# A forward loop in two-step order, halved products, writes moved to SyncE, and leftover work spread over the steps

## The chip, the cores and the metric

The kernel runs on one core of a Trainium2 chip, in one launch. The metric is the device time of that launch in microseconds, the median of several runs. One execution was also taken with the hardware profiler; its times are those of the tables and lines below. The engines are named as in the profile: PE (TensorE, matmuls), PEld (its weight loads), DVE (VectorE), ACT (ScalarE), POOL (GpSimd), SP (SyncE, which here only issues DMAs).

## The reference, cut to what matters

The kernel computes the forward output and all gradients of two attention blocks whose outputs are put side by side. `S` is 2048, `D` is 448, there are 16 heads of 28.

```
A: q, k, v = split(x_A @ wqkv);  phi(t) = where(t > 0, t + 1, exp(t)) + 1e-6
   o = (phi(q) @ (phi(k).T @ v)) / (phi(q) . sum(phi(k)) + 1e-6);  a = o @ wo        (linear attention)
B: q = x_B @ wq (16 heads);  k = x_B @ wk, v = x_B @ wv (one head for all)
   p = softmax(q @ k.T * 28 ** -0.5);  o = p @ v;  b = o @ wo                        (multi-query attention)
out = concat([a, b]);  returned: out and the gradients of all 8 inputs for a given grad_out
```

## The kernel before, in words

Block B sets the frame. A short start projects its queries, keys and values. Then comes the **forward loop** of 256 steps: 4 chunks of 512 queries (`qc`) x 4 groups of 4 heads (`g`) x 16 tiles of 128 keys (`t`). Step `s` does this, in this order:

- `act_e(2s)`, `act_e(2s+1)`: ACT takes the exponential of two score tiles (two heads each, 128 x 1024) from PSUM into the tile `e` of the step. `e` has five buffers.
- what earlier steps left in `posts`, among it the `phi` of block A's projections.
- `pe_s(2s+2)`, `pe_s(2s+3)`: PE computes the score tiles of the next step, two row-tiled matmuls each. The score tiles have two PSUM buffers, so `pe_s(2s+2)` waits for `act_e(2s)` and `pe_s(2s+3)` for `act_e(2s+1)`.
- `pe_o(s-1)`: PE adds `e` times the values of the step before into `oacc` (four column-tiled matmuls); SP then writes that `e` to the DRAM scratch `edram`, for the backward. After 16 steps DVE copies `oacc` out, and `o_tail` is put first in the list `fillers`.
- `block(1.15, 1.65)`: other work for PE and DVE.

Each engine carries out its instructions in the order in which the program issues them; the whole loop stands under a manual schedule. `block` is a small planner. It adds 1.15 to a budget (held to at most 1.65) and then takes pieces from the front of its lists, each with a written cost in about microseconds of PE, as long as the budget is at least half the next cost and the costs taken in this step stay within 1.65. One piece a step may come from `fillers` (what follows from the forward of B: `o_tail`, and after each `qc` the list of `queue_mid` with `o_tr`, `out_mm`, `do_mm`, `do_tr`), the others from `later` (the rest of B's projections) and then from `apools["q"]`: **all of block A, linear attention, forward and backward**, cut into pieces by `pieces_A`. These are, in order: projections with `phi` (ACT exponentials); `G_part` and others; `p3_...` per 128 rows (output, and the gradients towards `q`, `k`, `v`); `gwo`, whose last round writes `out_3` with 16 small DMAs from POOL (L391); `gwv`, `Wp`, `Zf`; `gw_all`, that is the weight gradients `gw` with 16 matmuls for each of four column blocks, cut in four pieces of 0.86; `p5_...` per 128 rows; and `gw` again for the keys. PSUM for all these pieces is a pool `gen` of three buffers; DVE evacuates them.

When `apools["q"]` is empty, `prefetch` closes block A's memory, and loads what the backward of B needs first. The **backward loop** of 256 units follows, then a tail with the weight gradients of B. Neither is touched.

Of the kernel before, what the change touches and what calls it, by code (L numbers as in the profile page):

```python
# [16 lines left out]
DH = 28  # L17
D = 448
P = 128
# [5 lines left out]
def kernel(  # L25
# [58 lines left out]
    def mm(out_ap, lhsT, rhs, start=True, stop=True):  # L84
        nc.tensor.matmul(out_ap, lhsT=lhsT, rhs=rhs, start=start, stop=stop, tile_position=(0, 0))  # L85
# [46 lines left out]
    def pieces_A(gen, pl, post, flush, pre_tiles, pk_d, early):  # L132
        slabs, halves, w4, accp, chk, small, awk = pl
        out = []

        def piece(cost):
            def add(fn):
                out.append((cost, fn))
                return fn
            return add  # L140

# [234 lines left out]
        def gwo(qc, g):  # L376
            ps = gen([P, D], "gwo_ps")
            for b in range(4):
                mm(ps[:, :], V["onat"][:, qc * 4 + b, g * P:(g + 1) * P], V["ga", qc][:, b, 0:D], start=(b == 0),
                   stop=(b == 3))  # L380
            acc = V["gwo"][:, g, :]
            if qc == 0:
                nc.vector.tensor_copy(out=acc, in_=ps[:, :])
            elif qc < NQC - 1:
                nc.vector.tensor_tensor(out=acc, in0=ps[:, :], in1=acc, op=ALU.add)
            else:
                gsb = awk.tile([P, D], BF16, name="gwoA_sb", tag="osbA", bufs=4)
                nc.vector.tensor_tensor(out=gsb[:], in0=ps[:, :], in1=acc, op=ALU.add)
                for j in range(4):
                    h = 4 * g + j  # L390
                    nc.gpsimd.dma_start(out_3[h * DH:(h + 1) * DH, :], gsb[32 * j + 1:32 * j + 1 + DH, :])  # L391
            if g == 3 and qc < 2:
                ga_load(qc + 2)

# [14 lines left out]
        def part_pk2(k):  # L409
            nc.gpsimd.dma_start(V["onat"][:, 2 * k:2 * k + 2, :].rearrange("p t c -> p (t c)"),  # L410
                                pk_d[:, 1024 * k:1024 * k + 1024])
# [71 lines left out]
        def gw(src, c, q, bi):  # L483
            if q == 0:
                V["acc"] = gen([P, 512], "gw_acc")
            acc = V["acc"]
            for st in range(4 * q, 4 * q + 4):
                mm(acc[:, :], V["x"][:, st, c * P:(c + 1) * P], V[src][:, st, :], start=(st == 0), stop=(st == NS - 1))
            if q == 3:
                out_gw(acc, c, bi)  # L490

        def gw_all(c):
            for q in range(4):
                piece(0.86)(lambda c=c, q=q: gw("gq", c, q, 0))
                if c in (1, 2) and q % 2 == 1:
                    piece(0.0)(lambda k=2 + 2 * c + q // 2: part_pk2(k))

        for c in range(4):
            piece(0.25)(lambda c=c: gwv(c))
# [35 lines left out]
            piece(0.25)(lambda g=g: wT_tr("k", g))  # L535
        gw_all(3)

        def p5_dp(i):
            if i % 4 == 1 and i // 4 < 3:
                xT2(i // 4 + 1)  # L540
            ps = gen([P, 512], "ps_dpk")
            for c in range(4):
                mm(ps[:, :], V["xT", i // 4][:, i % 4, c, :], V["Wp"][:, c, :], start=(c == 0), stop=(c == 3))
            dph = awk.tile([P, 512], BF16, name="dph_A")
            nc.vector.tensor_scalar(out=dph[:], in0=V["pk"][:, i, :], scalar1=-1e-6, scalar2=1.0, op0=ALU.add,
                                    op1=ALU.min)
            gk = awk.tile([P, 512], BF16, name="gk_A", tag="gnd", bufs=4)
            nc.vector.tensor_tensor(out=gk[:], in0=ps[:, :], in1=dph[:], op=ALU.mult)
            V["gk", i] = gk

        def p5_tr(i):
            ps = gen([P, 1024], "qk_ps", BF16)
            tr4(ps, lambda g: V["gq"][:, i, g * P:(g + 1) * P])
            tr4(ps, lambda g: V["pk"][:, i, g * P:(g + 1) * P], 4)
            a = awk.tile([P, 1024], BF16, name="qkT_A", tag="t2k", bufs=4)
            nc.vector.tensor_copy(out=a[:], in_=ps[:, :])
            V["a", i] = a
# [10 lines left out]
        def p5_gx(i, k):  # L568
            a, b = V["a", i], V["b", i]
            if k == 0:  # L570
                V["gx"] = gen([P, D], "ps_gx")
            ps = V["gx"]
            lhs = (a[:, 0:512], b[:], a[:, 512:1024])[k]
            rhs = (V["wT", "q"], V["wT", "k"], V["Z"])[k]
            for g in range(4):
                mm(ps[:, :], lhs[:, g * P:(g + 1) * P], rhs[:, g, :], start=(k == 0 and g == 0),
                   stop=(k == 2 and g == 3))
            if k == 2:
                ot = awk.tile([P, D], BF16, name="gx_sb", tag="osbA", bufs=4)
                nc.vector.tensor_copy(out=ot[:], in_=ps[:, :])  # L580
                nc.gpsimd.dma_start(out1[i * P:(i + 1) * P, :], ot[:])
                del V["a", i], V["b", i]

        for i in range(NS + 2):
            if 0 <= i - 1 < NS:
                piece(0.45)(lambda i=i - 1: p5_tr(i))
            if i < NS:
                piece(0.86)(lambda i=i: p5_dp(i))
            if 0 <= i - 1 < NS:
                piece(0.25)(lambda i=i - 1: p5_tk(i))  # L590
            if 0 <= i - 2:
                for k in range(3):
                    piece(0.76)(lambda i=i - 2, k=k: p5_gx(i, k))
        for c in range(4):
            for q in range(4):
                if q % 2 == 0 and c < 4 and 2 * c + q // 2 in early:
                    piece(0.0)(early[2 * c + q // 2])
                piece(0.86)(lambda c=c, q=q: gw("pk", c, q, 1))
        return out

    ps = ExitStack()
# [267 lines left out]
    def e_rows(g, qc):  # L869
        return (g * NQC + qc) * S  # L870
# [17 lines left out]
    def act_e(h):  # L888
        s, hf = divmod(h, 2)
        if hf == 0:  # L890
# [2 lines left out]
                             in_=sps.pop(h)[:].rearrange("p j (a q) -> p j a q", a=4), func=ACT.Exp,  # L893
                             scale=scale)

    def o_tail(qc, g, osb):
        otp = gen([P, 4, P], "otp")
        for b in range(4):
            tpz(otp[:, b, :], osb[:, b * P:(b + 1) * P], identF)
        otv = otp[:].rearrange("p b (j c) -> p b j c", c=32)  # L900
        rl = rls[qc]
        nc.vector.reciprocal(out=rl[:, :, 4 * g:4 * g + 4], in_=otv[:, :, :, 0])
        for b in range(4):
            nc.vector.tensor_tensor(
                out=hv(onats[qc][:, b, g * P:(g + 1) * P]),
                in0=otv[:, b], in1=rl[:, b, 4 * g:4 * g + 4].unsqueeze(2).to_broadcast([P, 4, 32]),
                op=ALU.mult)

    def pe_o(s):
        qc, g, t = steps[s]  # L910
        if t == 0:
            oaccs[0] = psAcc.tile([P, 512], F32, name="oacc", tag="acc")
            if g == 0:
                onats[qc] = mid2.tile([P, 4, 512], BF16, name="onat_q")
                rls[qc] = mid2.tile([P, 4, H], F32, name="rl_q")
        oacc = oaccs[0]
        e = es.pop(s)
        for j in range(4):
            cmm(oacc[32 * j:32 * j + 32, :].rearrange("p (a q) -> p a q", a=4), vaug[:, t, :],
                e[:, :, j, :], j, t == 0, t == NS - 1)  # L920
        r0 = e_rows(g, qc) + t * P
        nc.sync.dma_start(edram[r0:r0 + P, :], e[:].rearrange("p a j q -> p (a j q)"))
        if t == NS - 1:
            osb = fwk.tile([P, 512], F32, name="osb")
            nc.vector.tensor_copy(out=osb[:], in_=oacc[:, :])  # L925
            posts.append(lambda: posts.append(lambda: fillers.insert(0, (1.0, lambda: o_tail(qc, g, osb)))))
            if g == 3:
                posts.append(lambda: posts.append(lambda: queue_mid(qc)))

# [142 lines left out]
    def block(rate, cap):  # L1072
        budget[0] = min(budget[0] + rate, cap)
        used = 0.0
        while True:
            q = peek()
            if q is None:
                return
            cost = q[0][0]
            if used > 0 and used + cost > cap or budget[0] < 0.5 * cost:  # L1080
                return
            if q is fillers:
                turn[0] += 1
            q.pop(0)[1]()
            budget[0] -= cost
            used += cost

    closed = []
    loads = [(0, lambda k=k: load_q(0, (k,))) for k in range(3)]
# [13 lines left out]
    for s in range(NF):  # L1103
        turn[0] = 0
        act_e(2 * s)
        act_e(2 * s + 1)
        pend, posts[:] = posts[:], []
        for fn in pend:
            fn()
        pe_s(2 * s + 2)  # L1110
        pe_s(2 * s + 3)
        if s == NF - 1:
            pe_dp(0)
            pe_dp(1)
        if s > 0:
            pe_o(s - 1)
        block(1.15, 1.65)
        if apools.get("q") == []:
            prefetch(s)
    pe_o(NF - 1)  # L1120
    flush()
    flush()
# [229 lines left out]
```

## Time and profile before

| | us |
|---|---|
| median of 3 runs | 1327.22 |
| lowest, highest run | 1321.48, 1327.4 |
| the profiled execution's time | 1328.86 |
| its span, first to last instruction | 1327.0 |
| PE busy | 1238.0 |
| ACT busy | 1058.0 |
| DVE busy | 938.4 |

A line of the profile names the source line, the engine, the operation, the tile written and those read, the shapes, and then either `x` the number of instructions with the busy time, the mean of one in ns and the idle time before them, or, in views in order of time, start and length in us at the front and, in brackets, how long the engine had been idle and what ended that. Matmuls are pipelined, and weight loads overlap them, so a busy PE is not PE at its peak. "PEclk" is the share of TensorE's clock that was granted. L85, L89, L105 and L108 are lines of helpers that issue matmuls: the tile tells them apart.

### The profile page before, as it was taken

How to read it: one execution, taken by the hardware profiler on the slowest of the kernel's cores; microseconds unless marked ns; L12 is line 12 of the kernel's file. 1: busy time of each engine (PE TensorE's matmuls, PEld its weight loads, DVE VectorE, ACT ScalarE, POOL GpSimd, SP SyncE). 2: the span in 40 equal slices, each digit the busy share in tenths (PEclk: the TensorE clock that was granted, in tenths of full speed). 3: DMA queues.
4: the chain of work that ended last, by engine and by line, in shares of the span. 5: the costliest groups of instructions: out<-in, count | busy, mean ns of one | idle time of the engine just before them, and what ended most of it. 6: DMA issues, size and time to landing. Idle time of an engine off the chain costs nothing.

```text
span 1327.0 us, 30124 instructions
## 1 busy us (share of the span) xinstructions
PE 1238.0 (93%) x12604; PEld 589.7 (44%) x12604; DVE 938.4 (71%) x1243; ACT 1058.0 (80%) x1174; POOL 213.9 (16%) x305
## 2 busy tenths in 40 slices
PE   6988998889789999998999999999999999999988
PEld 2322233444333343322555555554555555555544
DVE  6854338888553446212889999998999999999921
ACT  3899987888678888896888888887888888888830
POOL 6400301111411111100031111111111111111110
PEclk8999999999899999995999999998999999999989
DMA  6887798886877787799999999999999999999661
GB/s 171 313 269 280 273 300 302 296 294 264 281 274 293 268 280 296 285 325 309 205 221 206 218 232 222 220 217 224 221 218 220 221 223 217 220 223 218 130 210 46
DMA packets 626312, 322.00 MB, mean 243 GB/s; under 512 B 579120, under 2 KB 585008, under 8 KB 625920
## 3 DMA queue, kind: packets, MB, share of 16 engines
q1 hardware_dynamic: 615072, 291.30, 85.3%
q0 software_dynamic: 10080, 28.73, 6.7%
q8 instruction: 98, 1.61, 0.5%
q14 instruction: 38, 0.31, 0.1%
q10 hardware_dynamic: 1024, 0.05, 0.0%
HBM read 21.87 MB, written 153.45 MB: 132 GB/s over the span
## 4 chain that ended last, share of the span: by engine, by line
PE 66%; DVE 3%; DMA 3%; ACT 3%; issue 2%; POOL 0%; ACTq 0%; DVEq 0%; POOLq 0%
PE dsT_ps L89 19%; PE dp_ps L105 12%; PE akv L108 10%; PE s_ps L105 5%; PE dq_ps L108 4%; PE oacc L108 3%; PE ps_gx L85 3%; PE gw_acc L85 2%; ACT e L892 2%; PE ps_dpk L85 1%; PE gwq_acc L85 1%; ACT dsT L1167 1%; PE gwoB_ps L85 1%; PE ps_gxB L85 1%; DVE ds L1145 1%
## 5 line engine op out<-in xcount | busy, mean ns | idle before, releaser
L1167 ACT ACTIVATE dsT<-dsT_ps 128x1024 bf16<-128x1024 bf16 x512 | 497.5, 1028 | 101.5 <-PE dsT_ps L89 96.0
L892 ACT ACTIVATE e<-s_ps 128x1024 bf16<-128x1024 f32 x512 | 496.8, 1056 | 89.2 <-ACT e L892 50.2
L1145 DVE TENSOR_TENSOR ds<-dp_ps,eN 128x1024 bf16<-128x1024 f32 x336 | 393.1, 1217 | 32.6 <-PE dp_ps L105 24.7
L89 PE MATMUL dsT_ps<-identB,ds 128*128 128x128 bf16 x4096 | 282.5, 221 | 0.5 <-DVE ds L1145 0.2
L89 PEld LDWEIGHTS <-ds 128*128 128x128 bf16 x4096 | 234.5, 98 | 64.0 <-issue 59.9
L1145 DVE TENSOR_TENSOR ds<-dp_ps,eN_h 128x1024 bf16<-128x1024 f32 x176 | 207.0, 1216 | 13.5 <-PE dp_ps L105 7.9
L105 PE MATMUL s_ps<-qT_B,kT_rep 32*128 32x512 bf16 x1024 | 170.4, 398 | 38.6 <-ACT e L892 36.3
L105 PE MATMUL dp_ps<-vT_rep,doT_b 32*128 32x512 bf16 x768 | 151.3, 390 | 7.2 <-DVE ds L1145 6.5
L108 PE MATMUL akv<-ds,qn_b 128*32 128x512 bf16 x1024 | 157.2, 387 | 0.0
L1197 POOL TENSOR_TENSOR dkv<-dkv,asb 128x512 f32<-128x512 f32 x60 | 76.4, 1273 | 493.2 <-ACT asb L1196 493.2
L105 PEld LDWEIGHTS <-kT_rep 32*128 32x128 bf16 x1024 | 43.7, 91 | 166.2 <-issue 155.4
L108 PE MATMUL oacc<-e,vaug 128*32 128x512 bf16 x1024 | 106.3, 406 | 0.8 <-DVE osb L925 0.8
L105 PEld LDWEIGHTS <-doT_b 32*128 32x128 bf16 x768 | 37.1, 91 | 107.5 <-issue 84.3
L108 PE MATMUL akv<-eN,don_b 128*32 128x512 bf16 x512 | 78.4, 386 | 0.0
L108 PE MATMUL dq_ps<-dsT,kn 128*32 128x512 bf16 x1024 | 66.8, 379 | 0.6 <-ACT dsT L1167 0.6
L108 PEld LDWEIGHTS <-vaug 128*32 128x32 bf16 x1024 | 26.5, 93 | 62.3 <-issue 62.3
L105 PE MATMUL dp_ps<-vT_rep,doT_q 32*128 32x512 bf16 x256 | 49.7, 385 | 0.0
L163 DVE TENSOR_SCALAR phi_ex<-phi_ex 128x512 f32<-128x512 f32 x32 | 13.7, 427 | 39.8 <-ACT phi_ex L162 39.8
L580 DVE CAST gx_sb<-ps_gx 128x448 bf16<-128x448 f32 x16 | 10.0, 624 | 44.9 <-PE ps_gx L85 44.9
L108 PEld LDWEIGHTS <-don_b 128*32 128x32 bf16 x768 | 22.0, 94 | 44.1 <-issue 44.1
L108 PEld LDWEIGHTS <-kn 128*32 128x32 bf16 x1024 | 27.8, 97 | 28.2 <-issue 0.4
L108 PE MATMUL akv<-eN_h,don_b 128*32 128x512 bf16 x256 | 39.8, 392 | 0.0
(283 smaller groups left out, 1270.2 us busy)
## 6 DMA issues: line engine op xcount, KB each, us to landing
edram<-e SPq DMA_DIRECT2D x256, 512.0 KB
pk_d<-pkn_A POOLq DMA_DIRECT2D x2, 1024.0 KB, 5.1
onat_d<-onat_q POOLq DMA_DIRECT2D x4, 512.0 KB, 4.5
onat_A<-pk_d POOLq DMA_DIRECT2D x8, 256.0 KB, 4.8
qn_b<-qn_d SPq DMA_DIRECT2D x4, 512.0 KB
onat_B<-onat_d SPq DMA_DIRECT2D x4, 512.0 KB
xa_nat<-in_A_x_dram POOLq DMA_DIRECT2D x1, 1792.0 KB, 12.3
ga_chunk<-in_grad_out_dram POOLq DMA_DIRECT2D x4, 448.0 KB, 6.3
```

What stands on the lines that cost most here:

```text
L85: nc.tensor.matmul(out_ap, lhsT=lhsT, rhs=rhs, start=start, stop=stop, tile_position=(0, 0))
L89: nc.tensor.transpose(out_ps_ap, in_ap, ident[0:k, 0:k], tile_position=(0, 0))
L105: nc.tensor.matmul(out_ap, lhsT=lhsT, rhs=rhs, start=True, stop=True, tile_position=(32 * j, 0))
L108: nc.tensor.matmul(out_ap, lhsT=lhsT, rhs=rhs, start=start, stop=stop, tile_position=(0, 32 * c))
L163: nc.vector.tensor_scalar(out=ex[:], in0=ex[:], scalar1=1.0, scalar2=1e-6, op0=ALU.min, op1=ALU.add)
L580: nc.vector.tensor_copy(out=ot[:], in_=ps[:, :])
L892: nc.scalar.activation(out=es[s][:].rearrange("p a j q -> p j a q")[:, 2 * hf:2 * hf + 2], in_=sps.pop(h)[:].rearrange("p j (a q) -> p j a ...
L1145: nc.vector.tensor_tensor(out=ds[:], in0=dps.pop(h)[:], in1=eNs[i][:, 2 * hf:2 * hf + 2, :], op=ALU.mult)
L1167: nc.scalar.activation(out=dsTs[kcu][:].rearrange("p t j q -> p j t q")[:, 2 * hf:2 * hf + 2, :, b * P:(b + 1) * P], in_=tps.pop(h)[:], fu ...
L1197: nc.gpsimd.tensor_tensor(out=dkv[:, kc * 512:(kc + 1) * 512], in0=dkv[:, kc * 512:(kc + 1) * 512], in1=asb[:], op=ALU.add)
```

## The change

- In the forward loop `pe_o` is no longer called once a step. In every even step, `pe_o(s-2)` and `pe_o(s-1)` come together, between `pe_s(2s+2)` and `pe_s(2s+3)`; odd steps have none.
- The write of `e` to `edram` becomes a function of its own, `write_e(s-1)`, called right behind the two `act_e`. It stays on SP.
- The 16 writes of `out_3` are issued by SP instead of POOL.
- The pieces of `gw`, `p5_dp` and `p5_gx` are cut in halves (0.43 and 0.38 each), and pieces may carry a limit of their own: these, with `p5_tr` and `p5_tk`, stop a step's block at 1.3 instead of 1.65. `o_tail` is priced 0.6 instead of 1.0.
- From step 128 the rate of `block` is no longer 1.15 but `pace(s)`: all that is left in the lists and still to come, divided by the steps up to step 246, plus 0.02, and at most 1.15.

```diff
-                    nc.gpsimd.dma_start(out_3[h * DH:(h + 1) * DH, :], gsb[32 * j + 1:32 * j + 1 + DH, :])
+                    nc.sync.dma_start(out_3[h * DH:(h + 1) * DH, :], gsb[32 * j + 1:32 * j + 1 + DH, :])
...
         def gw_all(c):
-            for q in range(4):
-                piece(0.86)(lambda c=c, q=q: gw("gq", c, q, 0))
+            for q in range(8):
+                piece(0.43, 1.3)(lambda c=c, q=q: gw("gq", c, q, 0))
...
-                piece(0.86)(lambda i=i: p5_dp(i))
+                piece(0.43, 1.3)(lambda i=i: p5_dp0(i))
+                piece(0.43, 1.3)(lambda i=i: p5_dp(i))
...
-                for k in range(3):
-                    piece(0.76)(lambda i=i - 2, k=k: p5_gx(i, k))
+                for k in range(6):
+                    piece(0.38, 1.3)(lambda i=i - 2, k=k: p5_gx(i, k))
...
+    def write_e(s):
+        qc, g, t = steps[s]
+        r0 = e_rows(g, qc) + t * P
+        nc.sync.dma_start(edram[r0:r0 + P, :], es[s][:].rearrange("p a j q -> p (a j q)"))
...
-            posts.append(lambda: posts.append(lambda: fillers.insert(0, (1.0, lambda: o_tail(qc, g, osb)))))
+            posts.append(lambda: posts.append(lambda: fillers.insert(0, (0.6, lambda: o_tail(qc, g, osb)))))
...
             cost = q[0][0]
-            if used > 0 and used + cost > cap or budget[0] < 0.5 * cost:
+            lim = q[0][2] if len(q[0]) > 2 and q[0][2] else cap
+            if used > 0 and used + cost > lim or budget[0] < 0.5 * cost:
...
+    def pace(s):
+        if s < 128:
+            return 1.15
+        left = sum(x[0] for x in apools["q"]) + sum(x[0] for x in fillers)
+        for qc in range(NQC - 1):
+            for g in range(4):
+                if s < qc * 64 + g * 16 + 18:
+                    left += 0.6
+            if s < qc * 64 + 66:
+                left += 4 * (0.25 + 0.76 + 0.86 + 0.25)
+        left += 0.6 * sum(1 for g in range(3) if s < (NQC - 1) * 64 + g * 16 + 18)
+        return min(1.15, left / max(NF - 10 - s, 1) + 0.02)
...
         act_e(2 * s)
         act_e(2 * s + 1)
+        if s > 0:
+            write_e(s - 1)
...
         pe_s(2 * s + 2)
+        if s % 2 == 0 and s > 0:
+            pe_o(s - 2)
+            pe_o(s - 1)
         pe_s(2 * s + 3)
...
-        if s > 0:
-            pe_o(s - 1)
-        block(1.15, 1.65)
+        block(pace(s), 1.65)
...
+    write_e(NF - 1)
+    pe_o(NF - 2)
     pe_o(NF - 1)
```

## The prediction

> **What bounds the kernel now.** I read the page first, then windows by stage, then the order of time inside two stretches. "Step" means one turn of the forward loop; the step starts come from the 512 `e` activations. Forward steps 0 to 255 run from 26.4 to 615.5 us (2.30 each), the backward loop and the tail after that.
>
> ```profile
> PE 1238.0 (93%) x12604; PEld 589.7 (44%) x12604; DVE 938.4 (71%) x1243; ACT 1058.0 (80%) x1174; POOL 213.9 (16%) x305
> L892 ACT ACTIVATE e<-s_ps 128x1024 bf16<-128x1024 f32 x512 | 496.8, 1056 | 89.2 <-ACT e L892 50.2
> ```
>
> The backward code isn't touched and its windows show PE at 25.00 of 25, so all is decided in the forward. There the `e` activations are the floor, but ACT sat idle 89.2 us before them.
>
> ```profile
> 100.00:125.00 25.00, 21.87 (x130) 6.64 (x128) 12.13 (x25) 24.22 (x32) 0.53 (x1) 0.93 0.79 289
> 225.00:250.00 25.00, 21.59 (x201) 10.34 (x198) 19.05 (x37) 20.53 (x22) 5.27 (x12) 1.00 0.78 285
> 350.00:375.00 25.00, 17.65 (x110) 6.78 (x107) 15.30 (x29) 11.95 (x13) 8.00 (x16) 0.81 0.65 248
> 550.00:575.00 25.00, 23.41 (x151) 7.64 (x149) 3.70 (x9) 22.61 (x25) 1.62 (x3) 1.00 0.95 297
> 575.00:600.00 25.00, 22.16 (x128) 6.39 (x127) 3.07 (x8) 23.48 (x25) 1.08 (x2) 0.81 1.05 353
> ```
>
> Columns: window, length, then busy PE, PEld, DVE, ACT, POOL, granted clock, DMA share, GB/s. At 100 ACT is full (`phi` shares it); at 225 neither PE nor ACT is full; at 350 both stand still. The ping-pong of the two is seen in order of time, PE alone and then ACT alone:
>
> ```profile
> 563.62 0.39 PE L105 MATMUL s_ps<-qT_B,kT_rep 32*128 32x512 bf16 x2 [0.21 <-ACT e L892]
> 563.94 0.40 PE L108 MATMUL oacc<-e,vaug 128*32 128x512 bf16 x4
> 564.27 1.04 PE L85 MATMUL gw_acc<-onat_A,pqT_A 128*128 128x512 bf16 x4
> 565.24 0.65 PE L105 MATMUL s_ps<-qT_B,kT_rep 32*128 32x512 bf16 x4
> 565.81 0.40 PE L108 MATMUL oacc<-e,vaug 128*32 128x512 bf16 x4
> 566.15 1.04 PE L85 MATMUL gw_acc<-onat_A,pqT_A 128*128 128x512 bf16 x4
> 567.12 0.39 PE L105 MATMUL s_ps<-qT_B,kT_rep 32*128 32x512 bf16 x2
> 567.71 0.39 PE L105 MATMUL s_ps<-qT_B,kT_rep 32*128 32x512 bf16 x2 [0.20 <-ACT e L892]
> ...
> 569.33 0.39 PE L105 MATMUL s_ps<-qT_B,kT_rep 32*128 32x512 bf16 x2
> ```
>
> ```profile
> 565.72 3.81 ACT L892 ACTIVATE e<-s_ps 128x1024 bf16<-128x1024 f32 x4 [0.28 <-ACT e L892]
> ```
>
> Constants, start to start: a score pair or four scores 0.33, oacc 0.33, a 0.86 product 0.97 (so filler F costs F + 0.11); one `e` 0.955; score start to `e` 0.48; `e` end to the next score 0.09. Two steps take 4.09 (565.24 to 569.33) where ACT needs 3.82: every second step PE blocks in front of the second pair until `e` ends, then comes late with the next scores.
>
> The stall at 350, on POOL's own timeline and then DVE's:
>
> ```profile
> 340.32 4.02 POOL L391 DMA_DIRECT2D out_dram<-gwoA_sb  x8 [4.28 <-DVE gwoA_sb L388]
> 348.56 0.57 POOL L952 DMA_DIRECT2D onat_d<-onat_q  x1 [4.22 <-issue]
> 349.12 2.01 POOL L391 DMA_DIRECT2D out_dram<-gwoA_sb  x4
> 351.12 0.55 POOL L961 DMA_DIRECT2D out_dram<-out_b_sb  x1
> ```
>
> ```profile
> 355.57 0.62 DVE L939 CAST out_b_sb<-ps_ob 128x448 bf16<-128x448 f32 x1 [6.62 <-DMA out_dram<-out_b_sb]
> ```
>
> The 16 small writes (8.04 us in all) plug POOL's queue, a two-buffer tile behind them isn't written out, DVE waits 6.62 us, and PE behind it 4.93.
>
> **The change part by part.** The sum is made against the profiled execution: 1328.86 us, span 1327.0 and 1.9 around it. The median of the three runs, 1327.22, lies 1.6 below.
>
> *Writes from SyncE.* Step 139 took 8.31 us and step 140, at half clock, 3.1, where 2.3 is usual: 6.8 over. With L391 gone from POOL, L952 and L961 go out when ready. I take -6 (bounds -5 and -7). On SP the same shape in the tail (L1307) takes 0.37 each: 16 x 0.37 = 5.9 us. It is hidden, since between 60 and 615 us SP waits for ACT's `e` for 357.6 us in all. The new wait, for `gwoA_sb` of DVE, has the `e` writes queued behind it; those free one of five buffers needed some 8 us later. Without that cover it costs the 5.9.
>
> *write_e* moves ahead of the score matmuls; nothing else stands between on SP: nothing.
>
> *Two-step order.* An even step is pair, two oacc groups, pair, F; an odd one four scores, F. Two adjacent oacc groups cost 0.33 + 0.21 (after 616 us, at half clock, eight took 1.04 against 0.62 for four: 0.42, halved): 0.55. Walk it with the constants at F = 1.0. Now: scores at 0, oacc 0.33, F 0.66, pair 1.77, second pair only at 2.48 (0.48 + 2 x 0.955 + 0.09), oacc 2.81, F 3.14, next scores 4.25: 2.125 a step. After: PE never waits, 4 x 0.33 + 0.55 + 2 x 1.11 = 4.09, and ACT's 3.82 fits inside: 2.045, so -0.08. In the same way at 0.86: 4.09 now (as measured), 3.94 after, -0.075; at 1.15: 4.40 to 4.22, -0.09. The oacc pair holds its `e` buffer one step longer, three steps before it is needed.
>
> Steps 16 to 47 are ACT-bound by `phi`: 0. Steps 0 to 15 and 48 to 63: -1.5 (0 to -2.4). Steps 64 to 127 take 2.36 where the walk gives 2.20, and DVE is 19 to 23 of 25 busy: I take -0.06 x 64 = -4 (0 to -5.8).
>
> The Trainium skill (TensorEngine Tiling, Key Properties) says that a change of tiling mode drains the array. The 0.11 agrees with it; there are six such changes in two steps before and after, so by that rule alone the order gains nothing, which is the first rival below.
>
> *o_tail at 0.6.* Behind the cheap tail step at 110.30 (0.66 of PE work) the clock fell to half: the next product took 1.87 at 112.62 against 1.04. Steps 36 and 52 took 3.6 for 2.3. A tail step now takes a product too: -2.6 (0 to -3.9).
>
> *Fine products and the even spread.* By the kernel's own budget rule walked over its list, steps 128 to 242 now carry 1.09 units each in lumps of 0.76 to 1.62, then 13 steps nothing. After, 128 to 245 carry 0.99, then ten nothing. (o_tail's price and an earlier list position make up the rest.) Before, the steps took 2.235 at 1.15 units (160 to 223) and 2.02 at 0.86: 0.73 per unit; my walk gives 0.53. I take 0.10 x 0.53 = 0.053 a step. With the order's 0.08 that is 0.13 x 115 = -15 (-6, if the order gives nothing, to -19). The light steps run at 1.98 either way.
>
> *DVE's pile-up.* Step 144 took 6.2: PE waited for evacuations of `Z_ps` and `do_mm`. By the list, Wp and Zf now come at 130 to 133, away from do_mm at 139 to 142, but with tail and gwv: some 10 us of DVE work in 8.2. So 4.4 goes and some 2 comes: -2 (+2 to -4; an accumulator held over ten blocks leaves two PSUM buffers).
>
> Sum: -6 - 1.5 - 4 - 2.6 - 15 - 2 = -31; 1328.9 - 31 = 1297.8, less 1.6 by the median: **1297**. DMA doesn't cap it: the forward now moves 289 GB/s for 588 us, 170 MB, which at the 353 seen at 575 takes 481 us, below the 555 that the forward would take.
>
> **The rivals.**
> *The order gives nothing,* stalls and spread do: -6 - 2 - 2.6 - 6 = -17, so 1328.9 - 17 - 1.6 = 1310. For it: DVE's load in 64 to 127.
> *PE's extra group decides (slower).* Even steps split the four scores: +0.33, less the 0.11 that joining oacc saves, 0.22 per two steps. Where PE waits less than that now, it is a loss: 0.11 x 224 = +25, less the 17 of the other parts, +8: 1328.9 + 8 - 1.6 = 1335. Against: at 225 PE idles 3.4 us in 11 steps, 0.62 per two; for it: lumps of 1.52 units leave none.
> *The thin steps lose the clock.* If PE's share falls as in the tail step (2.47 busy of the 3.41 us from 109.25, 72%), two steps at half clock take 4 x 0.54 + 0.96 + 2 x 2.1 = 7.3 (score to oacc took 0.54 at 358.68; a 0.86 product 1.80 at 372.70, so 2.1 for 0.99), 3.66 a step, +1.6. From 20 such steps of 118 all 31 is eaten; 25 give 1297 + 40 = 1337. Against: with 0.86 units PE works 95% of 4.09 and the clock stayed at 1.00. The Trainium skill (TensorE: Matmul & The Clock Gate, Part 1) has the gate watch a free-running window of 3413 ns and halve the clock after an idle one; the tail step agrees in length, though 72% busy was enough there to lose it.
> *It doesn't do what it says:* the stalls form again elsewhere or linear attention overruns step 246 and delays the first loads: -7 of 31 left, 1320 to 1327.
>
> **How the numbers follow.** Forecast 0.62, order nothing 0.15, no effect 0.08, extra group 0.10, clock 0.05. About 0.5% (6.6 us) is what a measurement of this kernel can tell from no change: faster 0.62 + 0.15 = 0.77, same 0.08, slower 0.10 + 0.05 = 0.15. All bounds at their best give -42 and some for p3's waits: 1284. Upwards the range takes in the second case and part of the fourth: 1320.
>
> **What would show it.** Steps 128 to 245 at 2.04 to 2.07 with hardly a step over 2.5; two oacc groups together every second step; no 5 us PE wait on `out_b_sb`; no granted clock below 1.00 between 125 and 580; L391 on SPq at some 0.37 each; backward as long as before, starting some 31 us earlier. Wrong, if steps 64 to 127 keep 2.36 and later ones 2.12, if PE waits for `e` between the two pairs of an even step, or if the windows from step 128 show a clock near 0.5.

## The result, and the profile after

The changed kernel takes **1312.28 us** (median of 4 runs, 1304.95 to 1314.53), the kernel before 1327.31 beside it: a ratio of 0.9855, 95% interval [0.9817, 0.9893]. The forecast was 1297, its range 1284 to 1320: faster, as said, but by half of what was said. The profiled execution took 1310.68 (span 1308.9), against 1328.86 before: 18.2 less, where the sum had 31.

The page of the changed kernel has the rows that were shown of before (`e` is L899 now):

```profile
PE 1226.3 (94%) x12546; PEld 584.9 (45%) x12604; DVE 938.2 (72%) x1243; ACT 1057.9 (81%) x1174; POOL 205.8 (16%) x289
...
L899 ACT ACTIVATE e<-s_ps 128x1024 bf16<-128x1024 f32 x512 | 499.2, 1075 | 70.8 <-ACT e L899 35.7
```

The same `e` work has 70.8 us of idle time before it, 18.4 less than before: nearly all of the gain. The windows, with the columns of the prediction (they hold the same times, not the same steps):

```profile
100.00:125.00 25.00, 21.68 (x129) 7.49 (x129) 13.34 (x28) 25.00 (x34) 0.55 (x1) 1.00 0.80 295
225.00:250.00 25.00, 23.73 (x201) 11.03 (x203) 18.43 (x39) 19.49 (x21) 5.35 (x11) 0.95 0.78 283
350.00:375.00 25.00, 24.42 (x167) 8.17 (x168) 14.57 (x28) 23.26 (x26) 5.19 (x9) 1.00 0.97 338
550.00:575.00 25.00, 24.05 (x153) 7.73 (x156) 3.70 (x9) 23.55 (x26) 1.62 (x3) 1.00 1.09 325
575.00:600.00 25.00, 17.05 (x98) 3.33 (x96) 1.15 (x2) 19.57 (x21) 0.55 (x1) 0.65 1.08 327
```

At 350 PE and ACT are both full now, where both stood still. At 225 PE is fuller and ACT emptier (19.49 for 20.53), and the clock has lost 0.05: that stage did not get better. The windows at 575 can't be compared: the last `e` of the changed kernel ends inside, at 597.8, that of the kernel before at 615.8. The order itself, on PE and then on ACT:

```profile
565.00 0.39 PE L105 MATMUL s_ps<-qT_B,kT_rep 32*128 32x512 bf16 x2
565.32 0.61 PE L108 MATMUL oacc<-e,vaug 128*32 128x512 bf16 x8
565.86 0.39 PE L105 MATMUL s_ps<-qT_B,kT_rep 32*128 32x512 bf16 x2
566.18 1.47 PE L85 MATMUL gw_acc<-onat_A,pqT_A 128*128 128x512 bf16 x6
567.59 0.39 PE L105 MATMUL s_ps<-qT_B,kT_rep 32*128 32x512 bf16 x4
567.91 1.04 PE L85 MATMUL gw_acc<-onat_A,pqT_A 128*128 128x512 bf16 x4
569.14 0.39 PE L105 MATMUL s_ps<-qT_B,kT_rep 32*128 32x512 bf16 x2 [0.19 <-ACT e L899]
```

```profile
561.71 5.71 ACT L899 ACTIVATE e<-s_ps 128x1024 bf16<-128x1024 f32 x6
```

A pair of scores, the two oacc groups (0.32 to 0.86, that is 0.54 start to start; the prediction had 0.55), a pair, filler, four scores, filler. PE doesn't wait between the two pairs of the even step (in steps 160 to 223 its idle time there is zero), and ACT did six `e` without a gap, where before it stopped after four.

By stage, in profiled executions (from the first `e` of one step to that of another; "start" is all before step 0, "rest" all from step 255 on):

| | before | after | forecast | measured |
|---|---|---|---|---|
| start | 26.7 | 28.7 | 0 | +2.0 |
| steps 0 to 63 | 148.7 | 146.9 | -1.5 - 2.6 | -1.8 |
| steps 64 to 127 | 151.2 | 155.5 | -4 | **+4.3** |
| steps 128 to 239 | 257.4 | 232.5 | -6 - 15 - 2 | -24.9 |
| steps 240 to 254 | 29.9 | 31.7 | 0 | +1.8 |
| rest | 713.2 | 713.6 | 0 | +0.4 |

The stage that was to bring most brought slightly more than forecast. The miss is 8.3 us in steps 64 to 127, and 2 each in the early steps, at the light end and in the start. But the border at step 128 has not the same work on its two sides before and after (see a4 below): steps 64 to 239 together brought 20.6 us where 27 were forecast. The start is scatter: kernels with the same code there took 26.1 to 28.8. In steps 64 to 127 there is hardly any: six kernels with the changed code there took 154.1 to 155.6. The rest holds scatter too: waits for a load in the middle of the backward, at another place from profile to profile and absent in three, cost 7.1 before (two of them) and 3.0 after (one).

### The profile page after: what moved, and what is told of

Its sections match the earlier page's. It is cut to its first block, busy times and chain, and to the rows that moved or that the text cites. A ratio compares the mean times of both kernels' runs of the same rounds, so it can differ in the third digit from the quotient of the medians.

```text
span 1308.9 us, 30065 instructions
## 1 busy us (share of the span) xinstructions
PE 1226.3 (94%) x12546; PEld 584.9 (45%) x12604; DVE 938.2 (72%) x1243; ACT 1057.9 (81%) x1174; POOL 205.8 (16%) x289
## 4 chain that ended last, share of the span: by engine, by line
PE 60%; DMA 3%; ACT 2%; issue 1%; DVE 1%; ACTq 0%; DVEq 0%
PE dsT_ps L89 19%; PE dp_ps L105 12%; PE akv L108 10%; PE dq_ps L108 4%; PE s_ps L105 4%; PE ps_gx L85 3%; PE oacc L108 2%; DMA eN_h<-edram 2%; ACT e L899 1%; PE gwq_acc L85 1%; PE gw_acc L85 1%; PE gwoB_ps L85 1%; DVE ds L1174 1%; PE ps_gxB L85 1%; PE ps_dpk L85 1%
## 5 line engine op out<-in xcount | busy, mean ns | idle before, releaser
L899 ACT ACTIVATE e<-s_ps 128x1024 bf16<-128x1024 f32 x512 | 499.2, 1075 | 70.8 <-ACT e L899 35.7
L1174 DVE TENSOR_TENSOR ds<-dp_ps,eN_h 128x1024 bf16<-128x1024 f32 x176 | 206.9, 1216 | 18.3 <-PE dp_ps L105 8.1
L105 PE MATMUL s_ps<-qT_B,kT_rep 32*128 32x512 bf16 x1024 | 186.1, 392 | 26.3 <-ACT e L899 20.8
L105 PEld LDWEIGHTS <-kT_rep 32*128 32x128 bf16 x1024 | 51.4, 91 | 188.3 <-issue 180.0
L108 PE MATMUL oacc<-e,vaug 128*32 128x512 bf16 x1024 | 81.3, 395 | 0.0
L108 PEld LDWEIGHTS <-don_b 128*32 128x32 bf16 x768 | 22.0, 94 | 44.2 <-issue 44.2
L1225 ACT ACTIVATE asb<-akv 128x512 f32<-128x512 f32 x60 | 36.2, 603 | 0.5 <-PE akv L108 0.5
```

Source lines behind the costliest of these rows:

```text
L105: nc.tensor.matmul(out_ap, lhsT=lhsT, rhs=rhs, start=True, stop=True, tile_position=(32 * j, 0))
L899: nc.scalar.activation(out=es[s][:].rearrange("p a j q -> p j a q")[:, 2 * hf:2 * hf + 2], in_=sps.pop(h)[:].rearrange("p j (a q) -> p j a ...
L1174: nc.vector.tensor_tensor(out=ds[:], in0=dps.pop(h)[:], in1=eNs[i][:, 2 * hf:2 * hf + 2, :], op=ALU.mult)
L1225: nc.scalar.activation(out=asb[:], in_=akv[:, :], func=ACT.Copy)
```

## The experiments

All stages in us; "units 0-15" are the first 16 units of the backward; 38.8 is what 16 later units take without a wait. Ratios are to the kernel before on the same chip.

| kernel | 64-127 | 128-143 | 144-159 | 128-239 | 240-254 | units 0-15 | span | ratio, interval |
|---|---|---|---|---|---|---|---|---|
| before | 151.2 | 42.5 | 39.5 | 257.4 | 29.9 | 45.8 | 1327.0 | |
| after | 155.5 | 37.9 | 32.4 | 232.5 | 31.7 | 49.9 | 1308.9 | 0.9855 [0.9817, 0.9893] |
| a1_order_undone | 154.9 | 37.4 | 34.6 | 242.1 | 30.8 | 45.2 | 1308.8 | 0.9919 [0.9893, 0.9944] |
| a2_six_buffers | 155.6 | 37.6 | 32.4 | 232.1 | 31.2 | 48.0 | 1305.1 | 0.9856 [0.9825, 0.9887] |
| a3_no_spread | 155.2 | 40.1 | 33.2 | 239.2 | 31.6 | 44.2 | 1304.1 | 0.9871 [0.9848, 0.9894] |
| a4_tail_dear_early | 149.7 | 36.9 | 38.0 | 239.3 | 31.7 | 49.5 | 1306.0 | 0.9855 [0.9829, 0.9881] |
| c1_light_dve | 141.7 | 38.9 | 32.4 | 233.5 | 31.6 | 46.3 | 1294.9 | one run |
| c2_light_dve_order_undone | 145.8 | 38.5 | 34.9 | 243.6 | 30.7 | 47.5 | 1309.0 | one run |
| c3_before_sp_writes | 151.0 | 38.2 | 38.2 | 251.8 | 29.8 | 44.2 | 1313.8 | 0.9965 [0.9946, 0.9983] |
| c4_end_early | 154.1 | 41.4 | 32.7 | 240.1 | 31.6 | 44.8 | 1309.7 | 0.9900 [0.9872, 0.9928] |
| d1_out3_spread | 155.4 | 34.9 | 34.9 | 232.0 | 32.0 | 47.8 | 1304.4 | 0.9843 [0.9816, 0.9870] |
| d3_out3_tail | 155.4 | 34.1 | 35.5 | 232.7 | 29.4 | 48.7 | 1300.7 | 0.9869 [0.9835, 0.9903] |
| e1_bounce | 155.5 | 34.2 | 33.0 | 229.4 | 31.6 | 49.6 | 1304.1 | 0.9867 [0.9843, 0.9890] |
| e2_bounce_tail | 150.1 | 34.6 | 37.2 | 236.0 | 31.6 | 49.9 | 1303.3 | 0.9853 [0.9831, 0.9874] |

### The order

**a1_order_undone**: the changed kernel with one `pe_o(s-1)` a step behind both score pairs again.

```diff
-        if s % 2 == 0 and s > 0:
-            pe_o(s - 2)
-            pe_o(s - 1)
         pe_s(2 * s + 3)
...
+        if s > 0:
+            pe_o(s - 1)
...
-    pe_o(NF - 2)
     pe_o(NF - 1)
```

> The changed kernel with the one-step order back (one oacc group in every step, behind the second score pair); everything else as changed. Stages are read from the starts of the e activations; changed kernel: steps 64 to 127 155.4 us, 128 to 143 37.9, 144 to 239 194.6. Theory (the order is worth some 0.08 us a step where PE and ACT alternate, nothing where DVE decides): 144 to 239 grows by 7 to 9 us, 64 to 127 stays within 2 us and keeps the slow pair of steps 82 and 83, the whole is 8 to 11 us slower than the changed kernel (some 1321). Rival 1 (the order is worth nothing, the lighter and more even steps did all): 144 to 239 within 2 us, the whole within 3 us. Rival 2 (the split of the four scores costs PE where it is full): 64 to 127 falls by 5 us or more, to 150 or less.

Steps 128 to 239 went from 232.5 to 242.1, so the order is worth 9.6 us there, 0.086 a step. By time it is 0.0064 of 1325, some 8.5 us. (The two spans are equal because the changed kernel's own profile had 2.3 more in the start and lost 9 us from step 255 on.) The wait that the order removes is back in its trace:

```profile
569.60 0.39 PE L105 MATMUL s_ps<-qT_B,kT_rep 32*128 32x512 bf16 x2 [0.46 <-ACT e L899]
```

In steps 64 to 127 the order was worth nothing, 154.9 against 155.5. That needed a cause of its own.

### Steps 64 to 127

Steps 82 and 83 took 4.4 and 4.6 us in the changed kernel. PE there, in order of time:

```profile
218.31 0.38 PE L89 MATMUL doT_ps<-identB,don_q 128*128 128x128 bf16 x4 [0.49 <-DVE gnd_A L321]
220.09 0.61 PE L368 MATMUL dkvz_ps<-gnd_A,oq_A 128*128 128x128 bf16 x8 [1.40 <-DVE gndT_A L342]
221.08 0.58 PE L85 MATMUL ps_nd<-kvz_blk,pqT_A 128*128 128x128 bf16 x4 [0.39 <-DVE gq_A L361]
```

PE waits three times for DVE, which worked without a gap from 210.75 to 223: it had `do_mm`'s products (L984 to L992), `osb` and a round of `p3` to do one behind the other. Behind the waits the clock was granted at half from 220.8 to 227.7.

**c1_light_dve**: the changed kernel without two DVE instructions of each `p3` round, the product with the output and its sum over each head (the gradient of the denominator is left out).

```diff
-            prod = awk.tile([P, 512], F32, name="prodA", bufs=1)
-            nc.vector.scalar_tensor_tensor(out=prod[:], in0=gnd[:], scalar=-1.0, in1=V["onat"][:, i, :], op0=ALU.mult,
-                                           op1=ALU.mult)
-            with nc.allow_low_precision("bf16 gradient of the denominator"):
-                nc.vector.tensor_reduce(out=hv(gnd[:])[:, :, 0], in_=hv(prod[:]), axis=AX.X, op=ALU.add)
```

> The changed kernel without two of the DVE operations of p3_go (the product with onat and its reduction, 32 instructions, some 20 us of DVE in steps 64 to 127); the denominator's part of the gradient is left out, so the output isn't the reference's. Theory (DVE decides steps 64 to 127): the stage falls from 155.5 us by 8 or more, to 147 or less, and the slow pair of steps 82 and 83 goes. Rival (PE's sum with the split scores decides there): within 3 us.

**c2_light_dve_order_undone** is c1 with the edit of a1 besides.

> The same with the one-step order back. With all of DVE's work the order made no difference in steps 64 to 127 (155.5 against 154.9). Theory (DVE hid the order's gain there): with the lighter DVE the one-step order is 3 to 6 us slower than the two-step order in this stage (0.05 to 0.09 a step). Rival (lumps of 1.5 units leave nothing to gain): within 1.5 us.

With the lighter DVE the stage fell by 13.8 us to 141.7 and the slow pair went. The long wait is gone from the same place, with `gnd_A` still awaited:

```profile
216.70 0.38 PE L89 MATMUL doT_ps<-identB,don_q 128*128 128x128 bf16 x4 [0.48 <-DVE gnd_A L321]
217.03 0.61 PE L363 MATMUL dkvz_ps<-gnd_A,oq_A 128*128 128x128 bf16 x8
```

With the light DVE the order is worth 145.8 - 141.7 = 4.1 us (one profile each), with the full one nothing: DVE hid it. So the prediction's -4 was right for a stage that PE and ACT bound, and in this one PE's waits for DVE decide.

**a4_tail_dear_early**: `o_tail` priced 1.0 as before, up to step 127.

```diff
-            posts.append(lambda: posts.append(lambda: fillers.insert(0, (0.6, lambda: o_tail(qc, g, osb)))))
+            posts.append(lambda: posts.append(lambda: fillers.insert(0, (1.0 if s < 127 else 0.6, lambda: o_tail(qc, g, osb)))))
```

> The changed kernel with o_tail priced 1.0 until step 127 and 0.6 after, so that up to step 127 the order of the pieces is that of the kernel before. Theory (the cheaper o_tail brought the p3 pieces three steps forward, into the steps of do_mm, and DVE's pile-up there makes the slow pair 82 and 83): no pair over 4 us near step 82, steps 64 to 127 fall from 155.4 to 149 to 152; the half-clock steps behind the tails of steps 34 and 50 come back (+2.6), and the spread steps carry 1.04 to 1.08 units for 0.99 (+3 to 5), so the whole is within 3 us of the changed kernel. Rival (the two-step order itself slows 64 to 127): that stage stays at 154 or more.

The stage fell from 155.5 to 149.7, and the slow pair went (81 and 84 took 3.2 and 3.3, for 2.9 and 3.5 before the change). The cheaper tail hands out more pieces per step, so that `p3`'s rounds come some five steps earlier: the first three begin in steps 68, 70 and 74 instead of 73, 80 and 82. Two things follow. One is the slow pair: a round meets `do_mm` and `osb`, and DVE has 18.3 us of work in the 20.9 of steps 77 to 83, where a4 has 15.5 in 16.1. The other is that work moves over the border at step 128. Steps 64 to 127 of the changed kernel and of a4, with DVE as the third busy time:

```profile
175.73:331.18 155.45, 138.88 (x1189) 63.98 (x1201) 123.60 (x257) 123.20 (x129) 26.46 (x57) 0.98 0.83 281
174.12:323.85 149.73, 133.95 (x1164) 61.80 (x1176) 117.01 (x245) 122.45 (x129) 22.25 (x50) 1.00 0.84 292
```

DVE has 6.6 us more to do there than in a4, and 7.4 less in steps 128 to 159 (36.1 for 43.6). So the 5.8 us of this stage are for the most part moved and not lost: steps 64 to 159 take 225.7 in the changed kernel, 224.6 in a4 and 233.2 before. Behind, a4 is slower (steps 137, 138 took 3.5 each, 144, 145 took 4.0 and 4.3), and the whole is no faster (0.9855). In a4 DVE has as much to do in steps 64 to 127 as before the change (117.2), so 151.2 - 149.7 = 1.5 is what the order gives there with the full DVE; with the list moved it gave nothing (a1).

**d3_out3_tail**: d1 (below) with the price of 1.0 for the tails before step 33 alone.

```diff
-            posts.append(lambda: posts.append(lambda: fillers.insert(0, (0.6, lambda: o_tail(qc, g, osb)))))
+            posts.append(lambda: posts.append(lambda: fillers.insert(0, (1.0 if s < 33 else 0.6, lambda: o_tail(qc, g, osb)))))
```

> The kernel of d1_out3_spread with o_tail priced at 1.0 again in forward steps before 33, so that p3's pieces don't move up into the do_mm steps 75 to 78. Theory (the moved-up pieces overload VectorE there): besides d1's gain, steps 64 to 127 fall from 155.5 us to 149 to 151 and the pair 82 and 83 of 4.4 and 4.6 us goes, whole about 1302 to 1304. Rival (the pair comes from the two-step order or the even start, not from where p3 starts): the pair stays at over 4 us each and the stage within 1.5 of 155.5.

The theory missed: 155.4, and steps 81 and 83 took 4.3 and 4.8. The list had moved (rounds at 70, 73, 81 and 83), but now a round stood at step 81 with `osb`. So it isn't "earlier" alone that makes the slow pair but which rounds fall on steps 81 to 83.

### The writes of `out_3`

**c3_before_sp_writes**: the kernel before with this one line of the change.

```diff
-                    nc.gpsimd.dma_start(out_3[h * DH:(h + 1) * DH, :], gsb[32 * j + 1:32 * j + 1 + DH, :])
+                    nc.sync.dma_start(out_3[h * DH:(h + 1) * DH, :], gsb[32 * j + 1:32 * j + 1 + DH, :])
```

> The kernel before with only the 16 out_3 writes moved from POOL to SP. Before, steps 139 and 140 took 8.3 and 3.1 us, 128 to 143 42.5, 144 to 159 39.5. Forecast of the prediction: 6 us off 128 to 143, nothing back. Theory now (the writes hold SP for some 8 us, among gbT transposes, and the e writes behind them come late): the stall at 139 goes, but 2 to 4 us come back as waits of ACT for a buffer of e or of DVE for an output tile; stage 128 to 159 falls by 2 to 5 us from 82.0. Rival (DVE's pile-up takes the place): within 1.5 us.

Steps 128 to 159 fell from 82.0 to 76.4, -5.6, as the prediction had it (-6): step 139 from 8.3 to 3.3 and 144 from 6.2 to 4.8. By time it is 0.9965 [0.9946, 0.9983], some 4.6 us. In the changed kernel, though, the writes made a wait of their own. SP's queue, then DVE and PE:

```profile
333.68 2.01 SPq L391 DMA_DIRECT2D out_dram<-gwoA_sb  x4
...
336.24 4.62 SPq L391 DMA_DIRECT2D out_dram<-gwoA_sb  x8
340.97 1.66 SPq L906 DMA_DIRECT2D edram<-e  x3
```

```profile
340.72 0.62 DVE L458 CAST gwA_sb<-gwv_ps 128x448 bf16<-128x448 f32 x1 [3.17 <-DMA out_dram<-gwA_sb]
```

```profile
341.40 0.38 PE L85 MATMUL Wp_ps<-dkvzT_blk,wTv_A 128*128 128x128 bf16 x4 [2.39 <-DVE gwA_sb L458]
```

`gwoA_sb` and `gwA_sb` share four buffers. By the order of the tiles DVE waits 3.17 us for the buffer of the third `gwoA_sb`, whose four writes stand among the eight from 336.24 on, and not for the `gwA_sb` that the line names (that is inferred from the order); PE waits 2.39 behind it, and step 131 took 4.6 us.

**a2_six_buffers**: six buffers instead of four for that tile (`tag="osbA", bufs=4` to `bufs=6`, in the four places that use it).

> The changed kernel with six instead of four buffers for the small output tiles (out_a_sb, gwoA_sb, gwA_sb, gx_sb share them). Theory (the stall of step 131 is the two last gwA_sb waiting for a buffer that the 16 out_3 writes, now one behind the other on SP, still hold): DVE's wait of 3.17 us and PE's of 2.39 go, steps 128 to 143 fall from 37.9 by 3 to 4.5 us, the whole by the same, near 1308. Rival (DVE's pile-up of gwo, gwv, Wp and tail evacuations makes the stall, whatever the buffers): steps 131 to 133 keep 3 us or more over the usual, 128 to 143 within 1.5 us.

DVE's wait went, but the stage stayed: 37.6 for 37.9. ACT now stood still for a buffer of `e`, whose writes were queued behind the 16 and between the four transposes of `gbT_q` (L956, 8.4 us in all) that SP issues after them:

```profile
350.11 3.79 ACT L899 ACTIVATE e<-s_ps 128x1024 bf16<-128x1024 f32 x4 [2.53 <-DMA edram<-e]
```

So more buffers only pass the wait on. What is late is SP's queue.

**d1_out3_spread**: the 16 writes one at a time between the next 16 product pieces, from a tile of their own.

```diff
...
+        def out3(h):
+            nc.sync.dma_start(out_3[h * DH:(h + 1) * DH, :],
+                              V["gwoS"][32 * (h % 4) + 1:32 * (h % 4) + 1 + DH, h // 4, 0:D])
...
+                if c < 2:
+                    piece(0.0)(lambda h=8 * c + q: out3(h))
```

> The changed kernel with its 16 small out_3 writes handed to SyncE one at a time between the next 16 product pieces, from a tile of their own, instead of in four groups of four. Theory (SyncE's lateness is the root: the block of 16 writes delays the tile behind it and the e writes): steps 128 to 143 fall from 37.9 us to 33 to 35, with no step over 2.9 among 131 to 135, and the whole from 1312 to about 1308. Rival (the accumulation and evacuation of gwA themselves are late): the stage stays within 1.5 of 37.9 and the slow steps stay.

Steps 128 to 143 fell to 34.9, as the theory said, but steps 144 to 159 rose from 32.4 to 34.9: the writes stood there now, ACT waited 1.51 us at 375.86 (the profile names PE there, but by the semaphores of the trace the write of the `e` of five steps before, issued at 368.90, landed just then, at 375.75), and the sum over 128 to 239 is 232.0 for 232.5. The delay had moved with the writes.

**e1_bounce**: five larger transfers on POOL instead of 16 small ones on SP, one of the whole tile to a scratch in DRAM and later four from there.

```diff
...
+            if g == 3 and qc == NQC - 1:
+                nc.gpsimd.dma_start(gwo_d[:, :].rearrange("p (g d) -> p g d", g=4), V["gwoS"][:, :, 0:D])
...
+        def out3(g):
+            nc.gpsimd.dma_start(out_3[g * 4 * DH:(g + 1) * 4 * DH, :].rearrange("(j e) d -> j e d", j=4),
+                                gwo_d[:, g * D:(g + 1) * D].rearrange("(j r) d -> j r d", j=4)[:, 1:1 + DH, :])
...
+                if c == 1 and q % 2 == 0:
+                    piece(0.0)(lambda g=q // 2: out3(g))
```

> The changed kernel with out_3 written in five larger transfers on GpSimd's queue instead of 16 small ones on SyncE: one write of the whole tile to a scratch in DRAM, later four copies from there to out_3. Theory (the writes' time on SyncE makes the e writes late, wherever the 16 are put): steps 128 to 143 at 33 to 35 us as in d1_out3_spread and steps 144 to 159 at 32 to 33 as in the change itself, so steps 128 to 239 at 228 to 230 instead of 232 and the whole 1299 to 1304 in the profiled run. Rival (d1's slow steps 148 and 151 come from the linear-attention pieces there, not from SyncE): steps 144 to 159 stay at 34.5 or more.

Steps 128 to 143 took 34.2, 144 to 159 took 33.0, no step between 131 and 151 over 2.7, and steps 128 to 239 fell to 229.4. POOL's queue carries it in

```profile
336.36 0.73 POOL L393 DMA_DIRECT2D gwo_d<-gwoA_sb  x1 [7.69 <-DVE gwA_sb L458]
...
368.34 1.42 POOL L493 DMA_DIRECT2D out_dram<-gwo_d  x2
...
370.33 1.35 POOL L493 DMA_DIRECT2D out_dram<-gwo_d  x2
```

0.73 + 1.42 + 1.35 = 3.5 us. The profiled run was 1305.9, 2 over the expected. This is what settles the stage: not where the 16 stood but that they took SP's time. In the changed kernel that cost 232.5 - 229.4 = 3.1 us of the 5.6 won.

**e2_bounce_tail** is e1 with the price of a4.

> The kernel of e1_bounce with o_tail priced at 1.0 until step 127 as in a4_tail_dear_early. Theory (in a4 the gain of 6 us in steps 64 to 127 was given back at steps 137, 138, where the out_3 writes stand, and 144, 145, where Wp and Z pile up on VectorE): steps 64 to 127 at 149 to 151, no step over 3 at 137 and 138, steps 128 to 239 at 234 to 237 instead of 239, whole 1298 to 1302. Rival (each stage's slack is only moved): steps 128 to 239 stay at 239 and the whole at 1304 to 1306.

Both stages came as the theory had them, 150.1 and 236.0, with no step over 3 at 137 and 138 (136 took 3.3). The whole didn't follow: 1305.97 by the median, where 1298 to 1302 was expected and 1304 to 1306 was the rival's. Step 144 still took 4.4, and steps 64 to 239 take 386.1 where e1 takes 384.9: with the writes out of the way, the price moves time and gains none.

### The spread

**a3_no_spread**: the changed kernel with the old rate from step 128 on.

```diff
-        block(pace(s), 1.65)
+        block(1.15, 1.65)
```

> The changed kernel with the rate 1.15 in every step, so without the even spread; its list then ends at step 233 and some 22 steps stay empty. Theory (step time grows by some 0.5 us per unit of filler, empty steps take some 1.95): 128 to 233 carry 1.11 units instead of 0.99, 106 x 0.12 x 0.5 = 6 us more, and 12 more empty steps save 12 x 0.1 = 1: some 5 us slower, near 1317. Rival (forward steps are bound by PE's sum, so moving work between them changes nothing): within 2 us of the changed kernel. Rival 2 (fuller steps lose nothing, ACT is the floor and the ends run freely): 3 us or more faster.

The forward lost 6.7 us in steps 128 to 239, as the theory had it, but not only where it had it: step 131, at the writes of `out_3`, took 6.5 for 4.6, and clear of these, in steps 144 to 239, 4.4 were lost. The whole was not slower: the rest of the kernel got 9.4 shorter (704.2 for 713.6), 5.7 of it in units 0 to 15, and the times differ by 0.0016, some 2 us, less than the interval: the size that the first rival had, though not for its reason. Where the gain went is seen behind the forward, on DVE of the changed kernel:

```profile
630.91 2.36 DVE L1174 TENSOR_TENSOR ds<-dp_ps,eN_h 128x1024 bf16<-128x1024 f32 x2 [2.09 <-DMA eN_h<-edram]
636.63 2.36 DVE L1174 TENSOR_TENSOR ds<-dp_ps,eN_h 128x1024 bf16<-128x1024 f32 x2 [3.36 <-DMA eN_h<-edram]
```

The list ends at step 246 in the changed kernel and at 233 in a3, and the first loads of the backward stand in its last pieces and behind it. The windows from 580 to 600 us, the changed kernel's and then a3's:

```profile
580.00:600.00 20.00, 13.05 (x74) 2.34 (x71) 0.54 (x1) 14.74 (x16) 0.00 (x0) 0.57 1.07 344
```

```profile
580.00:600.00 20.00, 14.49 (x76) 2.63 (x77) 0.00 (x0) 18.09 (x21) 0.00 (x0) 0.50 0.77 280
```

The DMA share is 1.07 where a3 has 0.77, and ACT waits for the writes of `e`:

```profile
589.36 1.94 ACT L899 ACTIVATE e<-s_ps 128x1024 bf16<-128x1024 f32 x2 [1.44 <-DMA edram<-e]
```

The two loads that units 10 and 11 wait for are the next ones on SP, issued at 622.71 and 628.64. Counted from the first `ds`, SP is through with them after 24.8 and 31.5 us, in a3 after 20.3 and 27.2.

**c4_end_early**: the spread ends 12 steps earlier, and the four half loads go out four steps apart.

```diff
-        return min(1.15, left / max(NF - 10 - s, 1) + 0.02)
+        return min(1.15, left / max(NF - 22 - s, 1) + 0.02)
...
-    loads += [(NF - 5, lambda: load_half(2, 0)), (NF - 2, lambda: load_half(3, 0))]
-    loads += [(NF, lambda n=n: load_half(n, 1)) for n in (2, 3)]
+    loads += [(NF - 16 + 4 * i, lambda n=n, k=k: load_half(n, k)) for i, (n, k) in enumerate(((2, 0), (2, 1), (3, 0), (3, 1)))]
```

> The changed kernel with the spread ending at step 234 instead of 246, and the first loads of the backward (tiles 2 and 3 of e in two halves each) issued at steps 240, 244, 248 and 252 instead of 251, 254 and behind the loop. Theory (the spread to step 246 pushes load_q and load_half into the last ten steps, where the e writes take the DMA queues: ACT waits at 250 and 251, and units 9 to 11 of the backward wait for eN_h): steps 144 to 239 some 5 us slower than 194.6, but steps 250 and 251 at 2.0 and the backward's first 16 units at 44 us or less instead of 49.9; the whole 0 to 4 us faster than the changed kernel. Rival (the backward's first units are slow by the half clock alone): these units stay at 48 to 50 and the whole is 4 to 6 us slower.

Units 0 to 15 fell to 44.8, 5.1 less, and the wait for `eN_h` went, as in a3. So an earlier end of the list, with the loads earlier, takes that wait away. How long it is varies: kernels whose list ends at step 246 take 45.2 (a1) to 49.9 in these units, those where it ends at 241 or before 44.2 to 45.8. But steps 128 to 239 rose by 7.6, 3.5 of it in steps 128 to 143, where the higher rate met the writes of `out_3` (step 131 took 5.3). By time it is 0.9900 [0.9872, 0.9928], an interval that overlaps with the changed kernel's: the expected gain didn't come.

No version beats the changed kernel by more than the measurement can tell. d1_out3_spread has the lowest ratio, 0.9843, whose interval overlaps with all the others' but those of a1, c3 and c4; e1's 3 us in the forward don't show in its median, and why they don't stays open. No run leaves out the halved pieces and their limit of 1.3 alone, so what they bring isn't known.

## Why the prediction was right or wrong

**What bounds the kernel** held: the gain is in the idle time before `e`, in the forward alone (20.5 us less in steps 0 to 254; start and rest came out 2.4 longer).

**Two-step order.** Right in its mechanism and size from step 128: 0.08 x 112 = 9.0 worked out, 9.6 by a1. What decided was PE's wait between the two pairs. The Trainium skill (TensorEngine Tiling, Key Properties) has a change of tiling mode drain the array; no run contradicts that, but what was worked out from it, that as many changes leave no gain, fell.

**Steps 64 to 127** is the step that failed: -4 was written, +4.3 came. The prediction had seen DVE busy 19 to 23 of 25 and still took two thirds of the walk's gain. Two things were missed. The order could give only 1.5 there, because PE waits for DVE (a4; c1 and c2 show it with 4.1 once DVE is lighter). And `o_tail` at 0.6, which was costed as a local gain, moves the whole list behind it: 5.8 (a4), in part as the slow pair of steps 82 and 83, for the most part as DVE work that steps 128 to 159 no longer have. So the -24.9 of the next stage was helped by this: with the list at its old place (a4) it brought 18.1 of the 23.

**o_tail at 0.6** (-2.6) and **steps 0 to 15 and 48 to 63** (-1.5) came out as -1.8 in all. The two slow steps 36 and 52 did go. But they also go with the old price under the new order (a4) and with the new price under the old order (a1), and in c3, with the price and the order of before, step 36 took 2.7 and not 3.6. The price wasn't needed.

**Writes from SyncE.** -5.6 against -6 in the kernel before (c3). In the changed one "hidden" was wrong: the prediction had 16 x 0.37 = 5.9 us on SP and compared it with SP's idle time over the whole forward. The 16 took 1.64 + 2.01 + 4.62 = 8.3, in a stretch of 9.4 us, and cost 3.1 (e1). The cover was an average and wasn't there where the writes stood; the 5.9 that the prediction gave for that case was too much.

**Spread and fine products.** The forward's part was right in kind: a3 loses 6.7 where 6 was written, but 4.4 of it clear of the writes of `out_3`, so the close agreement is partly luck. Steps 160 to 223 took 2.03 each, where 2.04 to 2.07 was written. What the sum put at nothing are the first loads, which come later with the end of the list (step 246; 241 before, 233 in a3): in units 0 to 15 +4.1 against before and +5.7 against a3. Steps 240 to 254 took 1.8 more than before, with ACT waiting for the writes of `e`; a3, without these waits, takes as long there, with its clock at half from 559.8 on, so what the late end costs in them isn't shown. "Backward as long as before" held (+0.4) only because the waits in its middle were shorter in this profile.

**DVE's pile-up**, -2: step 144 went from 6.2 to 1.8, and steps 131 to 133 rose in its place, as written; but that rise was SP's: in e1, with the writes off SP, the three took 7.1 for 10.8.

**The rivals.** Order nothing: fell (a1), though its price, 1310, is the one nearest to the 1312 that came; by the time alone one would have taken it for the right one. The forecast's own 1297 was 15 off; 1312 lies in the range because it had been widened upwards for the rivals. Extra group: fell; steps 128 to 239 are faster with the order, by 9.6 (a1) and by 10.1 (c1 against c2). Thin steps lose the clock: fell; between 450 and 550 us PE was busy 96.98 of 100 and the clock stayed at 1.00. The fourth, that stalls form again elsewhere, was right in kind (SP's queue, DVE at steps 82 and 83, the first loads), and so the clock did fall below 1.00 twice between 125 and 580; but all misses together took 13 of the 31 and not 24.

## What to carry to other kernels

Changing a written cost or rate in a planner moves all pieces behind it: before booking a local gain, list which pieces then stand in the same steps and add up their work on the second engine (here DVE), not on PE alone. For the same reason, compare the work in a stage along with its time: a stage can get slower because it has been given more to do. A queue's cover must be counted in the stretch where the instructions stand: 16 small writes made waits on POOL and on SP alike, five larger ones didn't. A faster stage whose end triggers loads gives part of it back there, so an even spread should be judged with the stage that follows.

## What the runs showed of the hardware that had not been expected

- Of the 16 small writes on SP, 13 took 0.32 to 0.40 us, like those in the tail (0.37); the other three took 0.74, 0.74 and 1.23, and the runs don't show why. On POOL before the change each took 0.51 to 0.53.
- The same `DMA_TRANSPOSE` of `eN` held SP 2.28 us at 592.38 in a3_no_spread and 6.62 at 587.23 in the changed kernel; the DMA share of the windows from 580 to 600 us was 0.77 and 1.07.
- The granted clock changed in steps of 3.41 us: half for 6.8 us from 220.8 and 3.4 from 343.7, each behind a PE wait (1.40 and 2.39 us), and for 27.3 from 582.6, once the list was empty. The Trainium skill (TensorE: Matmul & The Clock Gate, Part 1) names a window of 3413 ns, and the trace agrees.
